# Gated decode block: w_q's few-partition piece in 8 groups of 32 partitions, and a sigmoid made of exponentials

## The chip, the core and the metric

One core of one Trainium2 chip (trn2) runs the whole kernel in one launch. The metric is the device time of an execution in microseconds (us), as the median of several runs. Profiled executions are shown beside it: there the hardware profiler records every instruction and every DMA packet of one execution.

## The reference, cut to what matters

Two rows x (2 x 448) are normalised; one branch is attention of one new token over a cache of 4096 positions, the other a bilinear feed-forward part whose result goes through silu and gates the first.

```python
xn = (x - mean) / sqrt(var + 1e-5)                  # 2 x 448
q = xn @ wq                                         # 448 x 4096: 16 heads of 256, two for each of 8 kv heads
p = softmax(q @ k_cache.T / 16)                     # per row and kv head: 4096 positions of 256
s = (p @ v_cache) @ wo                              # 4096 x 448
g = silu(((xn @ w_gate) * (xn @ w_up)) @ w_down)    # silu(y) = y * sigmoid(y); 448 x 1792, twice, 1792 x 448
out = x + s * g
```

All is float32. The caches are 67 MB each, the weights some 25 MB: every byte is read once, and nearly all of the kernel's traffic is that.

## The kernel before, in words

**Data.** The host lays every input out so that a transfer is 128 partitions with one contiguous row each. There are 16 attention steps i, one for each pair of kv head and row of x; a step needs k_i and v_i, 4 MB each. They come in pairs "v_i k_(i+1)" into a ring of two 8 MB buffers (`ring`). Weights share one slot (`slot`, one buffer): w_q's first half with its extra piece, then w_gate and w_up, w_down with w_q's second half, then w_o. The last transfer (v15 and the last third of w_o, `wo2`) is cut in seven, so that its parts can be used as they land.

**Order of the transfers.** All of these are issued by SP, on one queue, in the order of a list written by hand (`plan`, and `issue`, which takes the next of the list; L78 issues a transfer, L82 the extra piece of w_q). The program calls `issue` behind the work that frees a buffer: the matmuls that read it stand ahead of the issue, and SP waits for them. x's two rows come on ACT's queue (L106).

**Start.** Layernorm of x on DVE (L118 to L130), transposes of xn on TensorE (L133, L155, L156) and copies that repeat a column 16 times for each row of x (L136): `xnT` holds 3 blocks of 128 rows of xn, `xf` the last 64 rows, `xeT` and `xl` pieces of these 64 rows for the extra piece of w_q.

**w_q's first half.** `rows` (L191) multiplies: four column tiles c, each with its own 32 columns of TensorE, and three blocks k of 128 rows (L199). The last 64 rows are folded: `block(12)` holds those of column tiles 0 and 1, 64 partitions each, and `block(13)` those of tiles 2 and 3 (L201). For the first half of w_q, block 12 is left out of the main transfer, which so is 13 x 512 wide, and comes as the piece `wqx`: tiles 0's and 1's 64 rows, as three parts of 20 rows for each (L208) and one of 4 + 4 rows (L211, with `xl`, which two selects of POOL have masked). Its transfer writes 20 partitions, 3584 numbers wide. Its source is made with shape 5 x 5 x 3584, of which `wqx[:, :4]` is read: 5 groups of 4 rows, with an unread row behind each group.

**A step.** `scores(i)` (L274) multiplies q with k_i and takes the maximum (L275); `softmax` (L287 to L298) makes it one maximum for all partitions, then ACT's exponential (L295) and a transpose on DVE; `values(i)` (L313) multiplies with v_i. After steps 0, 2, 4 and 8 a piece of other work is put in: the feed-forward's first half, its second half (`ffn_out`, L253 to L262), w_q's second half, and w_o's first part.

**The gate.** `ffn_out` multiplies with w_down (L256), sums over the tiles (`spread`, L239), and forms gate = y * sigmoid(y) from the 128 x 112 sums: ACT's sigmoid (L261) and a product on DVE (L262). The gate is read at the very end (L422).

**The end.** The last values() (L313, out to a tile `s`) reads v15 in three parts as they land; then ACT scales (L410), TensorE combines (L322) and multiplies with the last parts of w_o (`project`, L351, and `project_last`, L356), DVE multiplies by the gate and adds x (L422, L423), and SP stores the result.

Of the kernel before, what the change touches and what calls it, by code (L numbers as in the profile page):

```python
# [8 lines left out]
F32 = mybir.dt.float32  # L9
AF = mybir.ActivationFunctionType  # L10
OP = mybir.AluOpType
AX = mybir.AxisListType

B, D = 2, 448
HKV, REP, SK, DH = 8, 2, 4096, 256
F = 1792
NT = 4
W = 32
DUP = W // 2
NK = 4  # L20
# [3 lines left out]
SL = D // NT  # L24
# [2 lines left out]
LATE = 24  # L27
THIRD = [24, 25, 26, 28, 29, 30, 31, 27]
PART = 14 * (D + 512)
SIDE = 20  # L30
NS = 3
EXTRA = 2 * NS + 1
LEFT = 64 - NS * SIDE
EPS = 1e-5


# [5 lines left out]
def gated_decode_block(ctx: ExitStack, tc: tile.TileContext, x, first, vk, last0, last1, wq0, wqx, wdq, wo, wgu, out):  # L42
    nc = tc.nc
# [18 lines left out]
    loaded = {}  # L62
    todo = []

    def issue(n=1):
        for names, src, cuts in todo[:n]:
            weight = names[0].startswith("w")
            if weight:
                t = slot.tile([128, PART], F32, name="slot", align_bytes=512)
            else:  # L70
                t = ring.tile([128, 2 * ROW], F32, name="ring", align_bytes=512)
            width = ROW if not weight else src.shape[1] // len(names)
            for i, name in enumerate(names):
                loaded[name] = t[:, i * width:(i + 1) * width]
            if names == ["wd", "wq1"]:
                loaded["wd"], loaded["wq1"] = t[:, :14 * D], t[:, 14 * D:]
            for lo, hi in zip(cuts, cuts[1:]):
                nc.sync.dma_start(t[:, lo:hi], src[:, lo:hi])  # L78
            if names == ["wq0"]:
                at = src.shape[1]  # L80
                loaded["wqx"] = t[:, at:at + EXTRA * 512]
                nc.sync.dma_start(loaded["wqx"][:SIDE], wqx[:, :4])  # L82
        del todo[:n]

# [22 lines left out]
    ident = const.tile([128, 128], F32)  # L107
# [18 lines left out]

    xn = e1[:, 1]
    nc.vector.tensor_scalar(xn[:, :D], xc, rstd, None, op0=OP.mult)  # L128
    nc.vector.tensor_scalar(xn[:, D:D + LEFT], xc[:, D - LEFT:], rstd, None, op0=OP.mult)
    nc.vector.tensor_scalar(xn[:, D + LEFT:], xc[:, 384:D - LEFT], rstd, None, op0=OP.mult)  # L130
    pt = bank()
    for k in range(NK):
        nc.tensor.transpose(pt[:, B * k:B * (k + 1)], xn[:, k * 128:(k + 1) * 128], ident[:B, :B])  # L133
    def copies(dst, pt):
        n, b = pt.shape
        nc.vector.tensor_copy(dst.rearrange("p k (b j) -> p k b j", b=B),  # L136
                              pt.rearrange("p (k b) -> p k b", b=B)[:, :, :, None].to_broadcast([n, b // B, B, DUP]))
# [10 lines left out]
        half = slice(64 * a, 64 * (a + 1))  # L148
        copies(xf[half, a:a + 1], pt[half, (NK - 1) * B:NK * B])

    xeT = spare[:SIDE, :NS]
    pt = bank()
    for j in range(NS):
        at = 384 + j * SIDE
        nc.tensor.transpose(pt[:SIDE, B * j:B * (j + 1)], xn[:, at:at + SIDE], ident[:B, :B])  # L155
    nc.tensor.transpose(pt[:2 * LEFT, B * NS:B * (NS + 1)], xn[:, D - LEFT:D + LEFT], ident[:B, :B])  # L156
    copies(xeT, pt[:SIDE, :NS * B])

    xl = spare[:2 * LEFT, NK + 2:NK + 4]
    for a in range(2):  # L160
        copies(xl[:, a:a + 1], pt[:2 * LEFT, NS * B:(NS + 1) * B])
    nc.gpsimd.affine_select(out=xl, in_=xl, compare_op=OP.is_ge, fill=0.0, base=0, pattern=[[-LEFT, 2], [0, W]],
                            channel_multiplier=1)
    nc.gpsimd.affine_select(out=xl, in_=xl, compare_op=OP.is_ge, fill=0.0, base=LEFT - 1, pattern=[[LEFT, 2], [0, W]],
                            channel_multiplier=-1)

    both = work.tile([128, D], F32, name="h")[:B, :W].rearrange("p (b j) -> p b j", b=B)
    nc.vector.tensor_copy(both, ident[:B, :B, None].to_broadcast([B, B, DUP]))
# [22 lines left out]
    def rows(ps, w, n, extra=None):  # L191


        def block(i):
            return w[:, i * n:(i + 1) * n]

        for k in range(3):
            for c in range(NT):
                nc.tensor.matmul(ps[W * c:W * (c + 1), :n], xnT[:, k, :], block(NT * k + c), start=k == 0, stop=False)  # L199
        def last(a, i):  # L200
            nc.tensor.matmul(ps[64 * a:64 * (a + 1), :n], xf.rearrange("p a j -> p (a j)"), block(i), start=False, stop=True)  # L201

        if extra is not None:

            for j in range(NS):
                for c in range(2):
                    at = (c * NS + j) * n
                    nc.tensor.matmul(ps[W * c:W * (c + 1), :n], xeT[:, j, :], extra[:SIDE, at:at + n], start=False, stop=False)  # L208
                if j == 0:
                    last(1, 12)  # L210
            nc.tensor.matmul(ps[:2 * W, :n], xl.rearrange("p a j -> p (a j)"), extra[:2 * LEFT, 2 * NS * n:(2 * NS + 1) * n],  # L211
                             start=False, stop=True)
            return
        for a in range(2):
            last(a, 12 + a)


    qT = [const.tile([128, B, 4, 2, REP, DUP], F32, name=f"qT{h}") for h in range(2)]
# [33 lines left out]
    def ffn_out():  # L252
        ps = bank()  # L253
        for i in range(14):
            t = i % NT
            nc.tensor.matmul(ps[W * t:W * (t + 1), :D], hT[:, i], loaded["wd"][:, i * D:(i + 1) * D],  # L256
                             start=i < NT, stop=i >= 14 - NT)
        y = bank()
        spread(lift(ps), y, True, True)
        e = work.tile([128, D], F32, name="h")[:, :SL]  # L260
        nc.scalar.activation(e, y[:, :SL], AF.Sigmoid)  # L261
        nc.vector.tensor_mul(gate, y[:, :SL], e)  # L262


    def scores(i):
# [214 lines left out]
```

## Time and profile before

| | before |
|---|---|
| time, median of 3 runs | 376.34 us (376.27 to 376.48) |
| span of the profiled execution, first to last instruction | 374.6 us |
| bytes read from HBM | 158.56 MB, 423 GB/s over the span |
| TensorE: matmul busy, weight load busy | 197.4 us (53%), 55.3 us (15%) |
| DVE, ACT, POOL busy | 72.6, 25.8, 1.7 us |
| mean granted TensorE clock | 0.775 |
| main transfer of w_q's first half; its extra piece | 3328.0 KB; 280.0 KB |

The median is of executions that are timed without the profiler's records; the span is that of one other execution, and leaves out what lies ahead of the program's first instruction and behind its last. In the profile, a line such as "L313 PE MATMUL o<-ring,pT" reads: line 313 of the kernel, on TensorE, writes tile o from tiles ring and pT. "ring", "slot" and "last" are the names of buffers or inputs; buffer numbers are left out. DMA queues are q1 (what SP issues), q10 (what ACT issues), q8 and q14 ("instruction"). The core has sixteen DMA engines; a transfer of 128 partitions is shared by all of them, eight rows each, and a packet is here one row of a transfer.

### The profile page before, as it was taken

How to read it: one execution, taken by the hardware profiler on the slowest of the kernel's cores; microseconds unless marked ns; L12 is line 12 of the kernel's file. 1: busy time of each engine (PE TensorE's matmuls, PEld its weight loads, DVE VectorE, ACT ScalarE, POOL GpSimd, SP SyncE). 2: the span in 40 equal slices, each digit the busy share in tenths (PEclk: the TensorE clock that was granted, in tenths of full speed). 3: DMA queues.
4: the chain of work that ended last, by engine and by line, in shares of the span. 5: the costliest groups of instructions: out<-in, count | busy, mean ns of one | idle time of the engine just before them, and what ended most of it. 6: DMA issues, size and time to landing. Idle time of an engine off the chain costs nothing.

```text
span 374.6 us, 3092 instructions
## 1 busy us (share of the span) xinstructions
PE 197.4 (53%) x1388; PEld 55.3 (15%) x1388; DVE 72.6 (19%) x125; ACT 25.8 (7%) x40; POOL 1.7 (0%) x9
## 2 busy tenths in 40 slices
PE   0793459081726090858271756712718180909785
PEld 0210112020201020212020211200202020202122
DVE  2303030104040003040404050400211212030530
ACT  1001010001020002010101010100010101010121
POOL 0000000000000000000000000000000000000000
PEclk9968596778696587796778696885868586777999
DMA  8999899999999999999999999999999999999994
GB/s 327 435 493 434 376 438 441 448 443 437 431 428 443 441 434 420 422 427 434 436 448 448 427 426 397 452 448 448 436 427 420 436 427 420 448 411 441 411 416 186
DMA packets 4217, 158.81 MB, mean 424 GB/s; under 512 B 599, under 2 KB 857, under 8 KB 1241
## 3 DMA queue, kind: packets, MB, share of 16 engines
q1 hardware_dynamic: 4201, 158.62, 98.2%
q8 instruction: 11, 0.18, 0.2%
q10 hardware_dynamic: 4, 0.00, 0.0%
q14 instruction: 1, 0.01, 0.0%
HBM read 158.56 MB, written 0.06 MB: 423 GB/s over the span
## 4 chain that ended last, share of the span: by engine, by line
DMA 74%; PE 23%; issue 1%; DVE 1%; ACT 0%; POOL 0%; ACTq 0%; SPq 0%; DVEq 0%
DMA ring<-vk 67%; PE o L313 10%; PE s L274 8%; DMA ring<-last 5%; DMA p<-x 2%; PE s L199 1%; PE s L208 1%; PE s L313 1%; PE s L211 1%; PE s L356 0%; PE s L201 0%; PE wide L351 0%; ACT ob L410 0%; PE cb L322 0%; DVE pT L121 0%
## 5 line engine op out<-in xcount | busy, mean ns | idle before, releaser
L313 PE MATMUL o<-ring,pT 128*32 128x512 f32 x480 | 83.2, 856 | 115.6 <-DMA ring<-vk 115.6
L275 DVE TENSOR_REDUCE m<-s 128x1 f32<-128x1024 f32 x16 | 19.6, 1222 | 219.9 <-PE s L274 219.9
L274 PE MATMUL s<-ring,qT 128*32 128x512 f32 x512 | 59.6, 607 | 0.9 <-PE s L211 0.9
L313 PEld LDWEIGHTS o<-ring,pT 128*32 128x32 f32 x480 | 20.8, 150 | 168.6 <-issue 156.1
L295 ACT ACTIVATE p<-s,m 128x1024 f32<-128x1024 f32 x16 | 17.8, 1113 | 286.1 <-DVE m L293 286.1
L274 PEld LDWEIGHTS s<-ring,qT 128*32 128x32 f32 x512 | 17.2, 112 | 40.7 <-issue 38.1
L298 DVE STREAM_TRANSPOSE pT<-p 128x1024 f32<-128x1024 f32 x15 | 18.7, 1245 | 21.2 <-ACT p L295 21.2
L199 PE MATMUL s<-slot,xnT 128*32 128x512 f32 (+1 forms) x96 | 15.3, 788 | 3.3 <-DMA slot<-wgu 3.3
L287 PE MATMUL sm<-ident,m 128*1 128x128 f32 x16 | 4.3, 270 | 18.8 <-DVE m L275 18.8
L289 DVE TENSOR_REDUCE mx<-sm 1x128 f32<-1x512 f32 x16 | 10.7, 671 | 2.9 <-PE sm L287 2.9
L292 PE MATMUL sm<-one,mx 1*128 1x1 f32 x16 | 3.6, 226 | 14.2 <-DVE mx L289 14.2
L373 DVE COPY ob<-o 128x512 f32<-128x512 f32 x14 | 9.5, 681 | 0.0
L256 PE MATMUL s<-slot,hT 128*32 128x448 f32 x28 | 5.8, 918 | 4.4 <-DMA slot<-wdq 4.4
L351 PE MATMUL wide<-slot,oT 128*32 128x448 f32 x48 | 6.4, 684 | 0.7 <-DVE oT L340 0.6
L287 PEld LDWEIGHTS sm<-ident,m 128*1 128x1 f32 x16 | 1.3, 79 | 32.9 <-DVE m L275 32.3
L133 PE MATMUL s<-ident,pT 2*128 2x2 f32 x4 | 0.6, 246 | 10.4 <-DVE pT L128 10.4
L322 PE MATMUL cb<-ob,add_blocks 128*32 128x512 f32 (+2 forms) x48 | 4.1, 456 | 2.4 <-DVE ob L373 1.6
L199 PEld LDWEIGHTS s<-slot,xnT 128*32 128x32 f32 x96 | 3.5, 137 | 11.7 <-issue 11.7
L292 PEld LDWEIGHTS sm<-one,mx 1*128 1x128 f32 x16 | 2.3, 142 | 17.2 <-DVE mx L289 17.2
L295 ACT ACT_TABLE_LOAD x2 | 2.6, 1283 | 30.6 <-DVE m L293 23.5
L313 PE MATMUL s<-ring,slot 128*32 128x512 f32 x32 | 4.2, 600 | 0.8 <-DMA ring<-last 0.8
L201 PE MATMUL s<-slot,oT 128*64 128x448 f32 (+1 forms) x14 | 4.6, 664 | 0.0
(76 smaller groups left out, 47.5 us busy)
## 6 DMA issues: line engine op xcount, KB each, us to landing
ring<-last SPq DMA_DIRECT2D x2, 4096.0 KB, 24.8
slot<-wdq SPq DMA_DIRECT2D x1, 6720.0 KB, 45.5
slot<-wgu SPq DMA_DIRECT2D x1, 6272.0 KB, 32.7
slot<-wo SPq DMA_DIRECT2D x1, 5376.0 KB
ring<-first SPq DMA_DIRECT2D x1, 4096.0 KB, 20.6
slot<-wq SPq DMA_DIRECT2D x1, 3328.0 KB, 10.7
ring<-last SPq DMA_DIRECT2D x1, 2048.0 KB
ring<-last SPq DMA_DIRECT2D x1, 1536.0 KB, 17.8
```

Source lines behind the costliest of these rows:

```text
L199: nc.tensor.matmul(ps[W * c:W * (c + 1), :n], xnT[:, k, :], block(NT * k + c), start=k == 0, stop=False)
L256: nc.tensor.matmul(ps[W * t:W * (t + 1), :D], hT[:, i], loaded["wd"][:, i * D:(i + 1) * D], start=i < NT, stop=i >= 14 - NT)
L274: nc.tensor.matmul(s[W * c:W * (c + 1), h, :], q[:, d], k[:, h, d, c, :], start=d == 0, stop=d == 1)
L275: nc.vector.tensor_reduce(m[:, 0:1], s, axis=AX.XY, op=OP.max)
L287: nc.tensor.transpose(sm[:1, :128], m[:, 0:1], ident)
L289: nc.vector.tensor_reduce(mx, sm[:1, None, :128].rearrange("p o (c j) -> p o j c", c=NT).to_broadcast([1, NT, W, NT]), axis=AX.X, op=OP.max)
L292: nc.tensor.transpose(sm[:, 128:129], mx.rearrange("p c j -> p (c j)"), one)
L295: nc.scalar.activation(p, s, AF.Exp, bias=m[:, 1:2], scale=1.0 / 16, accum_out=su[:, place(i):place(i) + 1])
L298: nc.vector.transpose(pT.rearrange("p h n -> p (h n)"), p.rearrange("p h n -> p (h n)"))
L313: nc.tensor.matmul(o[W * t:W * (t + 1), :], pT[:, h, at:at + 2 * W:2], loaded[f"v{i}"][:, e * 512:(e + 1) * 512], start=e < NT, stop=e >= ...
L351: nc.tensor.matmul(wide[W * t:W * (t + 1), :D], heads(oT, i, first), w, start=i < NT, stop=i >= SIDES - NT)
L373: nc.vector.tensor_copy(ob[:, place(i) % 8], o)
```

## The change

- **The piece of w_q.** `SIDE` goes from 20 to 32 partitions, so the piece has 8 groups of 4 rows. It holds the last 64 rows of all four column tiles (two parts of 32 rows each) and, of block 11 (rows 256 to 383 of xn, column tile 3), the right half: 256 columns, as four parts of 32 rows. Its row is 5120 numbers. The main transfer of w_q's first half becomes 12 x 512 - 256 = 5888 numbers wide: blocks 12 and 13 and the half block are gone from it. No zeros are sent any more in place of rows that a part lacks.
- **Its operands and matmuls.** Six transposes of 32 rows each (two for the last 64 rows, four for rows 256 to 383) take the place of three of 20 and one of 8. `xl`, its two copies and POOL's two selects go. In `rows`, the last of the twelve main matmuls writes 256 columns; four matmuls of 256 columns and eight of 512 follow. Before it was twelve, six of 20 rows, one of block 13 and one of 4 + 4 rows.
- **The fold of the other weights** no longer rolls tiles 1's and 3's rows by four.
- **The gate.** With m = min(y, 0): sigmoid(y) = exp(m) / (1 + exp(2m - y)), where 2m - y is -|y|. DVE makes m and 2m - y side by side (128 x 112 each), ACT takes the exponential of both in one instruction, and DVE adds one, takes the reciprocal, and multiplies twice. ACT's program has one table load in place of three.

```diff
--- before.py
+++ after.py
@@ -27,10 +27,11 @@
 LATE = 24
 THIRD = [24, 25, 26, 28, 29, 30, 31, 27]
 PART = 14 * (D + 512)
-SIDE = 20
-NS = 3
-EXTRA = 2 * NS + 1
-LEFT = 64 - NS * SIDE
+SIDE = 32
+NS = 64 // SIDE
+HALF = 256
+QUARTERS = 128 // SIDE
+EXTRA = NT * NS * 512 + QUARTERS * HALF
 EPS = 1e-5
 
 
@@ -78,7 +79,7 @@
                 nc.sync.dma_start(t[:, lo:hi], src[:, lo:hi])
             if names == ["wq0"]:
                 at = src.shape[1]
-                loaded["wqx"] = t[:, at:at + EXTRA * 512]
+                loaded["wqx"] = t[:, at:at + EXTRA]
                 nc.sync.dma_start(loaded["wqx"][:SIDE], wqx[:, :4])
         del todo[:n]
 
@@ -126,8 +127,7 @@
 
     xn = e1[:, 1]
     nc.vector.tensor_scalar(xn[:, :D], xc, rstd, None, op0=OP.mult)
-    nc.vector.tensor_scalar(xn[:, D:D + LEFT], xc[:, D - LEFT:], rstd, None, op0=OP.mult)
-    nc.vector.tensor_scalar(xn[:, D + LEFT:], xc[:, 384:D - LEFT], rstd, None, op0=OP.mult)
+    nc.vector.tensor_scalar(xn[:, D:], xc[:, 384:], rstd, None, op0=OP.mult)
     pt = bank()
     for k in range(NK):
         nc.tensor.transpose(pt[:, B * k:B * (k + 1)], xn[:, k * 128:(k + 1) * 128], ident[:B, :B])
@@ -148,21 +148,12 @@
         half = slice(64 * a, 64 * (a + 1))
         copies(xf[half, a:a + 1], pt[half, (NK - 1) * B:NK * B])
 
-    xeT = spare[:SIDE, :NS]
+    xeT = spare[:SIDE, 6:6 + QUARTERS + NS]
     pt = bank()
-    for j in range(NS):
-        at = 384 + j * SIDE
+    for j in range(QUARTERS + NS):
+        at = 256 + j * SIDE
         nc.tensor.transpose(pt[:SIDE, B * j:B * (j + 1)], xn[:, at:at + SIDE], ident[:B, :B])
-    nc.tensor.transpose(pt[:2 * LEFT, B * NS:B * (NS + 1)], xn[:, D - LEFT:D + LEFT], ident[:B, :B])
-    copies(xeT, pt[:SIDE, :NS * B])
-
-    xl = spare[:2 * LEFT, NK + 2:NK + 4]
-    for a in range(2):
-        copies(xl[:, a:a + 1], pt[:2 * LEFT, NS * B:(NS + 1) * B])
-    nc.gpsimd.affine_select(out=xl, in_=xl, compare_op=OP.is_ge, fill=0.0, base=0, pattern=[[-LEFT, 2], [0, W]],
-                            channel_multiplier=1)
-    nc.gpsimd.affine_select(out=xl, in_=xl, compare_op=OP.is_ge, fill=0.0, base=LEFT - 1, pattern=[[LEFT, 2], [0, W]],
-                            channel_multiplier=-1)
+    copies(xeT, pt[:SIDE, :(QUARTERS + NS) * B])
 
     both = work.tile([128, D], F32, name="h")[:B, :W].rearrange("p (b j) -> p b j", b=B)
     nc.vector.tensor_copy(both, ident[:B, :B, None].to_broadcast([B, B, DUP]))
@@ -196,23 +187,20 @@
 
         for k in range(3):
             for c in range(NT):
-                nc.tensor.matmul(ps[W * c:W * (c + 1), :n], xnT[:, k, :], block(NT * k + c), start=k == 0, stop=False)
-        def last(a, i):
-            nc.tensor.matmul(ps[64 * a:64 * (a + 1), :n], xf.rearrange("p a j -> p (a j)"), block(i), start=False, stop=True)
-
+                part = HALF if extra is not None and (k, c) == (2, NT - 1) else n
+                nc.tensor.matmul(ps[W * c:W * (c + 1), :part], xnT[:, k, :], w[:, (NT * k + c) * n:(NT * k + c) * n + part], start=k == 0, stop=False)
         if extra is not None:
-
+            for j in range(QUARTERS):
+                at = NT * NS * n + j * HALF
+                nc.tensor.matmul(ps[W * (NT - 1):, HALF:n], xeT[:, j, :], extra[:SIDE, at:at + HALF], start=False, stop=False)
             for j in range(NS):
-                for c in range(2):
+                for c in range(NT):
                     at = (c * NS + j) * n
-                    nc.tensor.matmul(ps[W * c:W * (c + 1), :n], xeT[:, j, :], extra[:SIDE, at:at + n], start=False, stop=False)
-                if j == 0:
-                    last(1, 12)
-            nc.tensor.matmul(ps[:2 * W, :n], xl.rearrange("p a j -> p (a j)"), extra[:2 * LEFT, 2 * NS * n:(2 * NS + 1) * n],
-                             start=False, stop=True)
+                    nc.tensor.matmul(ps[W * c:W * (c + 1), :n], xeT[:, QUARTERS + j, :], extra[:SIDE, at:at + n], start=False,
+                                     stop=j == NS - 1)
             return
         for a in range(2):
-            last(a, 12 + a)
+            nc.tensor.matmul(ps[64 * a:64 * (a + 1), :n], xf.rearrange("p a j -> p (a j)"), block(12 + a), start=False, stop=True)
 
 
     qT = [const.tile([128, B, 4, 2, REP, DUP], F32, name=f"qT{h}") for h in range(2)]
@@ -257,9 +245,15 @@
                              start=i < NT, stop=i >= 14 - NT)
         y = bank()
         spread(lift(ps), y, True, True)
-        e = work.tile([128, D], F32, name="h")[:, :SL]
-        nc.scalar.activation(e, y[:, :SL], AF.Sigmoid)
-        nc.vector.tensor_mul(gate, y[:, :SL], e)
+        e = work.tile([128, D], F32, name="h")
+        up, low = e[:, :SL], e[:, SL:2 * SL]
+        nc.vector.tensor_scalar(up, y[:, :SL], 0.0, None, op0=OP.min)
+        nc.vector.scalar_tensor_tensor(low, up, 2.0, y[:, :SL], op0=OP.mult, op1=OP.subtract)
+        nc.scalar.activation(e[:, :2 * SL], e[:, :2 * SL], AF.Exp)
+        nc.vector.tensor_scalar(low, low, 1.0, None, op0=OP.add)
+        nc.vector.reciprocal(low, low)
+        nc.vector.tensor_mul(gate, y[:, :SL], up)
+        nc.vector.tensor_mul(gate, gate, low)
 
 
     def scores(i):
@@ -445,7 +439,7 @@
 
         full = w[:384].reshape(3, 128, NT, n).transpose(1, 0, 2, 3).reshape(128, 12, n)
         last = w[384:].reshape(64, 2, 2, n).transpose(2, 0, 1, 3)
-        last = np.concatenate([last[0], np.roll(last[1], LEFT, 0)])
+        last = np.concatenate([last[0], last[1]])
         return np.concatenate([full, last], 1).reshape(128, 14 * n)
 
 
@@ -453,14 +447,11 @@
     wq0, wq1 = [folded(wq[:, h], 512) for h in range(2)]
 
 
-    wqx = np.zeros((SIDE // 4, 5, EXTRA * 512), np.float32)
-    t0, t1 = wq0[:64, 12 * 512:13 * 512], wq0[64:, 12 * 512:13 * 512]
-    ends = np.zeros((SIDE, EXTRA, 512), np.float32)
-    ends[:, :NS] = t0[:NS * SIDE].reshape(NS, SIDE, 512).transpose(1, 0, 2)
-    ends[:, NS:2 * NS] = t1[LEFT:].reshape(NS, SIDE, 512).transpose(1, 0, 2)
-    ends[:2 * LEFT, 2 * NS] = np.concatenate([t0[NS * SIDE:], t1[:LEFT]])
-    wqx[:, :4] = ends.reshape(SIDE // 4, 4, EXTRA * 512)
-    wq0 = np.concatenate([wq0[:, :12 * 512], wq0[:, 13 * 512:]], 1)
+    wqx = np.zeros((SIDE // 4, 5, EXTRA), np.float32)
+    ends = wq[384:, 0].reshape(NS, SIDE, NT, 512).transpose(1, 2, 0, 3)
+    half = wq[256:384, 0, 4 * 512 - HALF:].reshape(QUARTERS, SIDE, HALF).transpose(1, 0, 2)
+    wqx[:, :4] = np.concatenate([ends.reshape(SIDE, -1), half.reshape(SIDE, -1)], 1).reshape(SIDE // 4, 4, EXTRA)
+    wq0 = c(wq0[:, :12 * 512 - HALF])
     wo = np.asarray(A_wo).reshape(NC, 128, D)[[*range(LATE), *THIRD]]
     wo = wo.transpose(1, 0, 2).reshape(128, NC * D)
     wo, last[1] = c(wo[:, :LATE * D]), np.concatenate([last[1], wo[:, LATE * D:]], 1)
```

## What I predicted

> **What bounds the kernel now.** I read the page first, then stretches of time, then the chain of waits.
>
> ```profile
> span 374.6 us, 3092 instructions
> PE 197.4 (53%) x1388; PEld 55.3 (15%) x1388; DVE 72.6 (19%) x125; ACT 25.8 (7%) x40; POOL 1.7 (0%) x9
> DMA packets 4217, 158.81 MB, mean 424 GB/s; under 512 B 599, under 2 KB 857, under 8 KB 1241
> q1 hardware_dynamic: 4201, 158.62, 98.2%
> q8 instruction: 11, 0.18, 0.2%
> q14 instruction: 1, 0.01, 0.0%
> DMA 74%; PE 23%; issue 1%; DVE 1%; ACT 0%; POOL 0%; ACTq 0%; SPq 0%; DVEq 0%
> ```
>
> No engine is busy for much over half of the span; SP's queue (q1) fills 98.2% of sixteen DMA engines, and 74% of the last chain is transfers. The stretches (columns: us, granted clock, share of the 16 engines, GB/s):
>
> ```profile
> 13.00:40.00 27.00, 0.79 1.03 445
> 40.00:365.00 325.00, 0.76 1.00 431
> 366.00:367.00 1.00, 1.00 1.02 420
> 367.62:368.90 1.28, 1.00 0.82 328
> 368.90:369.65 0.75, 1.00 0.58 222
> 369.65:370.20 0.55, 1.00 0.23 88
> 370.20:370.80 0.60, 1.00 0.08 30
> ```
>
> For 325 us all sixteen are full, at 431/16 = 26.9 GB/s each, so 1 us is 26.9 KB on one engine. At the end they do **not** stop together: the share falls to 0.82 (13 engines), 0.58 (9), 0.23 (4), 0.08 (1). A transfer has landed when its slowest engine has, so the others' spare time at the end is lost.
>
> Which engine stops late, and why, comes from the packets themselves. An engine's next packet starts where its last one ended (3 to 4 ns apart in the records), so 4201 packets fall into sixteen strings. No view prints these; I chained the trace's packet records, and numbers below that have no row are from there. The trace doesn't number the engines; grouped by what each carries, the strings end (us):
>
> ```
> carries                        strings  v's middle piece ends         last wo2 piece ends
> a w_q piece                       4     364.05 364.07 364.15 364.27   369.68 369.71 369.79 369.91
> a w_q piece, 8 KB instructions    1     364.67                        370.30
> neither                           3     361.98 362.00 362.23          367.62 367.64 367.87
> 16 KB instructions once           6     363.33 to 363.99              368.97 to 369.63
> 16 KB instructions twice          2     364.72 365.13                 370.36 370.77
> ```
>
> The few-partition piece of w_q is cut in 5 groups and lies on five strings, four packets of 14,336 B each. q8's first ten packets fall on eight other strings, in turn (the ninth and tenth on those of the first and second). Each leaves a hole of 0.86 to 0.95 us and makes the packet behind it some 0.5 us longer: 1.4 us. Three strings have neither.
>
> Does the end hang on the slowest string? The chain of waits, in order of time (start, us, what):
>
> ```profile
> 307.23 30.44 DMA ring<-vk
> 337.81 6.01 PE o L313 x32
> ...
> 347.69 17.79 DMA ring<-last
> 365.52 2.30 PE s L313 x16
> ...
> 370.09 0.78 PE s L356 x24
> 370.88 0.19 PE s L239 x8
> 371.07 0.47 PE s L356 x16
> ```
>
> And the timeline of PE ahead of the wait (start, us, ..., idle before and what ended it):
>
> ```profile
> 362.81 1.93 PE L313 MATMUL s<-ring,slot 128*32 128x512 f32 x16
> 365.52 2.28 PE L313 MATMUL s<-ring,slot 128*32 128x512 f32 x16 [0.79 <-DMA ring<-last]
> ```
>
> Yes, twice. The second half of the last values() waits 0.79 us for v's middle piece, whose last string ends at 365.13. The last eight passes of project_last start at 371.1, 0.33 us after the last string ends at 370.77; PE gets there at the same moment by the other way. Both instants are the slowest string's, and what follows (to 374.6) is fixed work.
>
> **The change part by part.**
>
> *w_q's piece.* Per string, main w_q goes from 8 x 26,624 B to 8 x 23,552 B: 24,576 B less, **-0.91 us** for all sixteen. The piece is now 32 rows of 20,480 B in 8 groups of 4: +81,920 B, +3.04 us, on eight strings. I take these to be the five that have a piece (which lose 57,344 B, 2.13 us) and the three that have nothing:
> - five with a piece: -0.91 - 2.13 + 3.04 = 0.00. Last end 370.30, the others by 369.91.
> - three with nothing: -0.91 + 3.04 = +2.13: 369.75, 369.77, 370.00.
> - eight with instructions: -0.91: 369.86 and 369.45 where there are two packets, the rest under 368.8.
>
> That the three new ones are these and not three others is the one premise. Five groups lay on five strings that had no q8 packet though eight of the sixteen had; q8 walks round a closed set of eight. [...]
>
> *The gate's sigmoid* (i = 2, after the fourth softmax). ACT loses two table loads; DVE has six operations in place of one:
>
> ```profile
> L295 ACT ACT_TABLE_LOAD x2 | 2.6, 1283 | 30.6 <-DVE m L293 23.5
> 109.30 1.28 ACT L261 ACT_TABLE_LOAD   x1
> ...
> 142.97 1.28 ACT L295 ACT_TABLE_LOAD   x1 [23.52 <-DVE m L293]
> ...
> 119.49 0.28 DVE L262 TENSOR_TENSOR gate<-s,h 128x112 f32<-128x112 f32 x1 [0.90 <-ACT h L261]
> 140.02 1.23 DVE L275 TENSOR_REDUCE m<-s 128x1 f32<-128x1024 f32 x1 [20.25 <-PE s L274]
> ...
> 140.01 29.93 DMA ring<-vk
> ```
>
> Five more at 0.28 us are 1.4 us, and DVE idles 20.25 us behind them: nothing. The load that returns to the exponential at 142.97 frees 1.28 us of softmax 4, whose reader waits for v4 until 169.94 by the chain: nothing. With those covers gone it would be +1.4 and -2.6 us.
>
> One thing could count. In 0 to 373 us there is one q14 packet:
>
> ```profile
> q14 instruction: 1, 0.01, 19.3%
> ```
>
> This is the stretch 108.70 to 108.80. It is 8,192 B at 108.75, 0.55 us ahead of the sigmoid's table load, and lies on the string that ends at 370.30: a hole of 0.30 us and a packet 0.53 us longer, 0.83 us. Without it that string ends at 369.47, and the three strings at up to 370.00 are last. If it belongs to the table load it goes; if it holds instructions of some engine, it stays. For "goes": the place, and that no other such packet is in the run. For "stays": the other two table loads have none; PE's 2776 recorded instructions took 11 packets of 16,384 B, 252 each, so 8,192 B are 126 instructions, and DVE runs 125 that are counted: about one such block must be fetched for it in the run, whatever ACT does. DVE has one instruction more after the change and three or four fewer ahead of this point, so its block would come as many DVE instructions later, at the same price. [...] Bounds: 0 (stays) and -0.30 us (goes). I take **0**: the count of instructions is nearer than one coincidence in time.
>
> *query(0).* Two transposes and six matmuls more, one of them half as wide, some with 32 rows; POOL's two selects go.
>
> ```profile
> 12.97 5.28 PE s L199 x24
> 22.36 1.91 PE s L211 x2
> 24.27 0.91 issue
> 25.18 5.36 PE s L274 x32
> 30.56 45.70 DMA ring<-vk
> ...
> 24.29 0.34 SPq L78 DMA_DIRECT2D slot<-wgu  x1
> ```
>
> Three rounds over four tiles took 5.28 us, 1.76 each. Now: three rounds (5.3), four half-width matmuls in one tile (at most half of 1.91 each, 3.8), two rounds of the last rows (3.5): 12.6 us against 11.3 from 12.97 to 24.27, so +1.3 at most, and below it down to -2 if the half blocks overlap. Behind it, SP's issue of w_gate/w_up moves from 24.29 to 25.6; the first string is through with v0 at 39.4, so 13 us cover it, and the vk issue at 30.56 is wanted at 54. DMA keeps full (1.03 in 13 to 40 us): nothing. PE's 24 instructions more move each q8 packet six matmuls earlier, on the same strings; ten still fall ahead of the end.
>
> *Sum.* The last string ends at 370.30 in place of 370.77: **-0.47 us**; v's middle piece at 364.67 in place of 365.13: -0.46. PE's first half of that values() ends at 364.74, so up to 0.78 us it is no new wait, and it starts from vk's last landing, which moves by the same. The profiled execution's span goes from 374.6 to 374.1. The median of the runs, 376.34, is 1.7 above the span, for what lies around it; the same difference gives **375.87**.
>
> **The rivals.**
> 1. *The 8 KB packet goes with the table load.* The last string is then 370.00: -0.77, **375.57**. For and against as above.
> 2. *The three newly loaded strings carry q8 packets.* That decides as soon as one of them does. The price is on that string: one with one packet goes to 369.63 + 2.13 = 371.76 (+0.99, 377.33), the worst with two to 372.90 (+2.13, **378.47**), and the end would wait there alone. Against: five of five avoid the eight so far, and just three are left. For: the trace has no engine numbers.
> 3. *It doesn't do what it says: the piece is spread over all sixteen.* 655,360 B / 16 = 40,960 B, 1.52 us each: the string with two packets goes to 370.77 - 0.91 + 1.52 = 371.38, +0.61, **376.95**. Against: 5 groups went to 5.
>
> **How the numbers follow.** Forecast 0.54, rival 1 0.35, rival 2 0.07, rival 3 0.04. Start times of the strings differ by over 1 us (first packets 1.8 to 3.3 us) and single packets by up to 0.08, so an end of one string is good to about 0.15 us. Predicted 375.87; range **375.4 to 376.1**: from rival 1 less 0.15 to the forecast plus 0.2; rivals 2 and 3 (0.11) and tails lie outside. 0.2% is 0.75 us, about what a measurement here can tell from no change: below 375.59 lies half of rival 1 and little else, 0.24; above 377.09 rival 2, 0.07; between, 0.69.
>
> **What would show it.** Right: 32 packets of 20,480 B, on eight strings, none of them with a 16 KB packet; shares at the end of 0.9 to 369.4 and then a steep fall; last string at 370.2 to 370.4; the wait ahead of the second half of values() still put down to a DMA, with PE ahead of it 0.5 us earlier. The q14 packet tells the forecast from rival 1: present behind 108.75, or gone, with the last string at 370.0. Wrong: a 20,480 B string with a 16 KB hole that ends past 371; a hole in the strings between 13 and 365 us that no instruction packet explains; or PE, not DMA, ahead of the last two waits.

## The result, and the profile after

The changed kernel takes **376.88 us** (median of 16 runs, 376.51 to 378.25) where the kernel before, run beside it, takes 376.23 us (16 runs, 376.00 to 376.90): a ratio of **1.0026, 95% interval 1.0018 to 1.0034**. It is slower by a quarter of a per cent; 375.87 had been predicted, with a range of 375.4 to 376.1. The 16 runs stand in two groups with nothing between them: nine at 376.51 to 376.88 and seven at 377.82 to 378.25. That split turns out to be part of the answer. The profiled execution is of the lower group: its own time is 376.88, its span 375.0 (before: 376.34 and 374.6).

The page of the changed kernel, the lines that answer to those shown of before:

```profile
span 375.0 us, 3108 instructions
PE 195.8 (52%) x1398; PEld 57.1 (15%) x1398; DVE 74.2 (20%) x127; ACT 23.4 (6%) x38; POOL 1.3 (0%) x7
DMA packets 4232, 158.78 MB, mean 423 GB/s; under 512 B 602, under 2 KB 860, under 8 KB 1244
q1 hardware_dynamic: 4216, 158.59, 98.1%
q8 instruction: 11, 0.18, 0.2%
q14 instruction: 1, 0.01, 0.0%
DMA 78%; PE 20%; issue 0%; SPq 0%; ACT 0%; DVE 0%
```

As many bytes, the same eleven q8 packets, the 8 KB packet of q14 still there, no engine much nearer to full (DVE 74.2 us for 72.6, weight loads 57.1 for 55.3, matmuls 195.8 for 197.4), and transfers hold more of the last chain (78% for 74%). Nothing here says why it is slower. The stretches do (columns: us, granted clock, share of the sixteen DMA engines, GB/s):

```profile
13.00:40.00 27.00, 0.76 1.02 441
40.00:365.00 325.00, 0.74 1.00 432
366.00:367.00 1.00, 1.00 1.02 420
367.62:368.90 1.28, 1.00 0.75 301
368.90:369.65 0.75, 1.00 0.62 241
369.65:370.20 0.55, 1.00 0.23 88
370.20:370.80 0.60, 1.00 0.16 60
370.80:371.20 0.40, 1.00 0.11 40
```

Up to 367 us the shares of the two profiles differ by 0.01 at most. A share of 0.9 had been forecast up to 369.4; instead it is 0.75 and then 0.62 (before: 0.82 and 0.58). After that, 0.16 x 16 = 2.6 and 0.11 x 16 = 1.8 strings go on, to 371.18, where before it was 0.08 x 16 = 1.3 and one string that ended last, at 370.77. Two strings are late, not one.

The same packet records as before, chained end to start, show which two (no view prints this; us):

```
carries                                 strings  middle piece of v ends     last wo2 piece ends
w_q piece only                             5     364.06 to 364.21           369.69 369.77 369.83 369.85 369.85
w_q piece, 8 KB instructions (110.91)      1     364.84                     370.48
w_q piece, 16 KB instructions once         2     365.49 365.54              371.13 371.18
nothing                                    2     -                          366.77 367.30
16 KB instructions once                    4     -                          368.22 368.26 368.32 368.57
16 KB instructions twice                   2     -                          369.23 369.51
```

The piece lies on eight strings as the diff says. Two of the eight are among those that carry PE's instruction packets (at 263.80 and 287.89 us, each with its hole of 0.86 us). The three that were to be filled up were not the three empty ones: two strings still have nothing, so only one of those three got the piece.

Does the end still hang on the last string? The chain of waits of the changed kernel, in order of time (start, us, what):

```profile
347.15 18.75 DMA ring<-last
365.94 2.31 PE s L307 x16
...
370.52 0.78 PE s L350 x24
371.30 0.19 PE s L227 x8
371.49 0.51 PE s L350 x16
```

and its timeline of PE (start, us, ..., idle before and what ended it; L307 is before's L313):

```profile
362.38 1.92 PE L307 MATMUL s<-ring,slot 128*32 128x512 f32 x16
365.94 2.29 PE L307 MATMUL s<-ring,slot 128*32 128x512 f32 x16 [1.65 <-DMA ring<-last]
```

PE arrives 0.43 us earlier than before (362.38 for 362.81) and starts the second half 0.42 us later (365.94 for 365.52): its idle time ahead of v's middle piece goes from 0.79 to 1.65 us. The last string's end moves by the same amount, 371.18 - 370.77 = +0.41, and so does the span, +0.4. From the last string's end to the kernel's time it is 376.34 - 370.77 = 5.57 us before and 376.88 - 371.18 = 5.70 after. That constant, 5.6 to 5.8 us, held in each of the nine experiments whose strings were read to the end, so one string's end gives the time.

### The profile page after: what moved, and what is told of

The parts are those of the page before. It is cut to its first block, busy times and chain, and to the rows that moved or that the text cites. A ratio compares the mean times of both kernels' runs of the same rounds, so it can differ in the third digit from the quotient of the medians.

```text
span 375.0 us, 3108 instructions
## 1 busy us (share of the span) xinstructions
PE 195.8 (52%) x1398; PEld 57.1 (15%) x1398; DVE 74.2 (20%) x127; ACT 23.4 (6%) x38; POOL 1.3 (0%) x7
## 4 chain that ended last, share of the span: by engine, by line
DMA 78%; PE 20%; issue 0%; SPq 0%; ACT 0%; DVE 0%
DMA ring<-vk 68%; PE o L307 11%; PE s L268 8%; DMA ring<-first 5%; DMA ring<-last 5%; PE s L307 1%; PE s L350 0%; SPq L83 0%; PE wide L345 0%; ACT ob L404 0%; PE cb L316 0%; SPq L79 0%; PE sm L300 0%; DVE gate L416 0%; DVE gate L417 0%
## 5 line engine op out<-in xcount | busy, mean ns | idle before, releaser
L307 PE MATMUL o<-ring,pT 128*32 128x512 f32 x480 | 84.2, 865 | 115.2 <-DMA ring<-vk 115.2
L307 PEld LDWEIGHTS o<-ring,pT 128*32 128x32 f32 x480 | 21.3, 150 | 168.0 <-issue 150.9
L191 PE MATMUL s<-slot,xnT 128*32 128x448 f32 (+2 forms) x96 | 16.3, 830 | 2.2 <-DMA slot<-wgu 2.2
L244 PE MATMUL s<-slot,hT 128*32 128x448 f32 x28 | 4.9, 811 | 5.4 <-DMA slot<-wdq 5.4
L316 PE MATMUL cb<-ob,add_blocks 128*32 128x512 f32 (+2 forms) x48 | 5.4, 575 | 2.4 <-DVE ob L367 1.6
L345 PE MATMUL wide<-slot,oT 128*32 128x448 f32 x48 | 4.9, 543 | 1.6 <-DMA slot<-wo 1.1
L307 PE MATMUL s<-ring,slot 128*32 128x512 f32 x32 | 4.2, 599 | 1.8 <-DMA ring<-last 1.6
L287 DVE TENSOR_SCALAR m<-sm 128x1 f32<-128x1 f32 x16 | 2.5, 159 | 5.1 <-PE sm L286 5.1
L212 DVE STREAM_TRANSPOSE qT<-s 128x256 f32<-128x256 f32 x4 | 1.6, 428 | 10.0 <-PE s L199 7.3
```

The costliest lines, as they stand in the source:

```text
L191: nc.tensor.matmul(ps[W * c:W * (c + 1), :part], xnT[:, k, :], w[:, (NT * k + c) * n:(NT * k + c) * n + part], start=k == 0, stop=False)
L307: nc.tensor.matmul(o[W * t:W * (t + 1), :], pT[:, h, at:at + 2 * W:2], loaded[f"v{i}"][:, e * 512:(e + 1) * 512], start=e < NT, stop=e >= ...
L316: nc.tensor.matmul(cb[W * c:W * (c + 1), :n * 64], add_blocks[:, e].rearrange("p r j -> p (r j)"), src[:, :n, e, :, c, :], start=e == 0, s ...
```

## The experiments

Theory after the result: the time is the end of the slowest string; every term of the sum has its predicted size, and only the assignment was wrong. Two engines carry both the piece and PE's 16 KB packets, and which engines get a second such packet differs from run to run; that makes the two groups. Rivals: the gate's exponentials cost time; the piece costs something besides its bytes; the two groups are a disturbance that has nothing to do with the kernel. None of the ten kernels leaves out any of the reference's work; e5 and e6 add matmuls, and e1 and e7 transfers, that nothing reads. A string is called doubled below when two 16 KB instruction packets fell on it, and the round is the set of engines on which these packets fall in turn.

### e2_gate_only: the gate's edit in the kernel before

```
-        e = work.tile([128, D], F32, name="h")[:, :SL]
-        nc.scalar.activation(e, y[:, :SL], AF.Sigmoid)
-        nc.vector.tensor_mul(gate, y[:, :SL], e)
+        up, low = e[:, :SL], e[:, SL:2 * SL]
...
+        nc.scalar.activation(e[:, :2 * SL], e[:, :2 * SL], AF.Exp)
...
```

> The kernel before with the gate made of exponentials alone. Theory (the piece of w_q costs, the gate nothing): as before, 376.2 us within 0.2, and the 8,192-byte packet is still there without a table load in the run. Rival (the gate's DVE work or a shift in the programs costs the difference): 376.9 us, slower by 0.6.

Measured: 376.28 (11 runs) beside 376.29 (21 runs), ratio 1.0003 (0.9994 to 1.0011). The profile of e2, ACT's table loads in its groups, and q14 in 0 to 373 us:

```profile
L301 ACT ACT_TABLE_LOAD x1 | 1.3, 1283 | 7.2 <-DMA p<-x 7.2
```

```profile
q14 instruction: 1, 0.01, 0.0%
```

One table load is left, in the kernel's first microseconds; the two around the gate are gone. The 8 KB packet is still there, at 110.86 us. So the gate's edit changes the time by no more than some 0.1% either way, and the packet does not belong to the gate's table loads.

### e3_piece_only: the changed kernel with its old sigmoid

```
-        nc.scalar.activation(e[:, :2 * SL], e[:, :2 * SL], AF.Exp)
...
+        nc.scalar.activation(e, y[:, :SL], AF.Sigmoid)
+        nc.vector.tensor_mul(gate, y[:, :SL], e)
```

> The changed kernel with the table's sigmoid back, so the new piece alone. Theory: as the changed kernel, most runs at 376.5 to 376.9 and a second group at 377.8 to 378.3, last string 371.2. Rival (the gate costs): 376.2 us in one group.

Measured: 376.67 (11 runs: eight from 376.58 to 376.85, then 377.20 and 378.18, and one of 411.71 at a granted clock of 1.0, which nothing here explains), ratio 1.0015 (1.0005 to 1.0024). The end of its DMA, columns as above:

```profile
370.20:370.60 0.40, 1.00 0.17 63
370.60:370.90 0.30, 1.00 0.13 48
```

Again two strings (0.13 x 16 = 2.1) go on alone, to 370.88 and 370.97, and they are two with the piece and one 16 KB packet each, here at 156.6 and 176.0 us instead of 263.8 and 287.9. The round of the q8 packets had started three strings further on. So the piece alone makes the loss, and the round does not start at the same string in every profiled run. The run of 377.20 lies between the two groups; it has no trace.

### e1_numbers and e7_numbers: which engine is which

The trace does not number engines. If a transfer of a few rows, n, leaves packets on n strings, and these are nested, small transfers of different n tell the strings apart. e1 puts fourteen of them (2 to 15 rows) behind the first vk:

```
+    probe = qT[1].rearrange("p b g d r j -> p (b g d r j)")
+    at = 0
+    for n in range(2, 16):
+        nc.sync.dma_start(probe[:n, at:at + 4 * n], first[:n, :4 * n])
+        at += 4 * n
```

> The changed kernel with fourteen tiny transfers behind the first vk (2 rows of 8 numbers, 3 rows of 12, up to 15 rows of 60, so packets of 32 to 240 bytes), which number the strings: string number e carries those of more than e rows. Nothing else changes, so about 376.9 or 378.0 us as the changed kernel shows. Theory (the piece now shares engines with instruction packets): the 20,480-byte packets lie on strings 0 to 7, two of the strings 5 to 7 carry a 16 KB packet each and end last (371.2 us), the eight strings with 16 KB packets are neighbours in number, and the two strings that end first (366.8, 367.3) have numbers over 7. Rival (the piece is not on the lowest strings, or instruction packets are dealt out anew in every program): the 16 KB packets are on strings without order, or not on 5 to 7.

Measured: 383.44 us; the probe was too large. The packets of the transfers of nine and more rows moved only at 43.2 to 45.8 us, and w_gate/w_up came behind them. SP's instructions on line 79 from 20 to 60 us (duration ns min/median/max, first and last start):

```profile
L79 SPq EVENT_SEMAPHORE  x4: 17/17/10471, 45.0 to 52.3; - x4
L79 SPq DMA_DIRECT2D slot<-wgu x1: 352/352/352, 45.0 to 45.0; - x1
```

In the changed kernel the slot<-wgu issue is at 21.28; here it is at 45.0, and everything behind it is late. Its time says nothing. Its strings could be read only in part: number 5 carried two 16 KB packets and number 6 one.

e7 keeps six of them:

```
+    for n in (5, 6, 7, 13, 14, 15):
```

> The changed kernel with six tiny transfers behind the first vk (5, 6, 7, 13, 14 and 15 rows: packets of 80, 96, 112, 208, 224, 240 bytes), few enough that SP isn't held up; 376.5 to 378.3 us. They tell string 5 (96 and 112 but not 80), 6 (112 alone of these), 7 (none of these three, but the piece), and 13, 14, 15. Theory: strings 6 and 7 carry instructions and 5 does not, and the two strings with nothing are 14 and 15, so that the round is 6 to 13. Rival: another two of 5 to 7, or a round that is not of neighbours.

Measured: 378.50 us, one run. The strings, by number (us):

```
number      piece   16 KB packets at         last wo2 piece ends
0 to 4      yes     none (one has 8 KB)
5           yes     two: 80.76, 355.92       372.71
6           yes     one: 106.97              371.08
7           yes     none                     369.83
8 to 12     no      one each on four; none on one (367.02)
13          no      one: 290.07
14          no      two: 46.27, 327.54       369.73
15          no      none                     367.96
```

The detail of my expectation was wrong: 5 and 6 carry packets, not 6 and 7, and the round isn't a block of neighbours. In time order the packets went to 14, 5, 6, four of 8 to 12, 13, and again to 14 and 5. The numbers are those of the probes: the transfers of 5, 6, 7, 13, 14 and 15 rows had packets on as many strings, each smaller one's strings were among the next one's, and the piece's eight groups lay on the strings so numbered 0 to 7.

This run is of the upper group, and shows how that comes about: string 5 carries the piece and **two** 16 KB packets. The end of e7's DMA:

```profile
370.80:371.10 0.30, 1.00 0.09 36
371.10:372.70 1.60, 1.00 0.06 25
```

From 371.10 on one single string (0.06 x 16 = 1) runs, for 1.6 us, until 372.7; the kernel's time, 378.50, is 5.79 us behind its end at 372.71.

### e5_after_more_instr and e6_before_more_instr: every engine of the round gets two

If the groups come from which engines get a second packet, then a kernel that fetches sixteen of them before the end, two for each of the eight engines, must have one group: the upper one with the change, and without it the upper end of before's spread. Both kernels add 32 one-element matmuls to twelve softmaxes (the page of e5 counts 768 matmuls and 768 weight loads more, 1536 instructions on PE):

```
+        if 1 <= i <= 12:
+            for n in range(32):
+                nc.tensor.matmul(sm[:1, 256 + n:257 + n], one, one, start=True, stop=True)
```

> The changed kernel with 32 tiny matmuls more in each of the softmaxes 1 to 12, whose results nobody reads: 1536 instructions of TensorE, six 16 KB packets more, 16 in all ahead of the end, so that each of the eight strings that carry them has two wherever the round starts. Theory (the two groups of runs of the changed kernel are starts of the round at different strings, the slow ones where a string with the piece has two packets): one group of runs, at the height of the slow one, last string 371.18 + 1.41 = 372.6, 378.0 to 378.3 us, and the two piece strings with instructions last in the trace. Rival (the instruction packets are not what holds the end): 376.5 to 376.9 and now and then 378, as without them.

> The kernel before with the same tiny matmuls. Theory: every one of its eight instruction strings has two packets; last is the one that starts latest, 369.63 + 1.41 = 371.0 in place of 370.77: 376.3 to 376.9 us. Rival (the matmuls themselves or their traffic delay the end): as much slower as the changed kernel gets by them, 1.3 us or more.

Measured, e5: 378.14 (four runs, 378.04 to 378.23), ratio 1.0051 (1.0034 to 1.0068); e6: 376.81 (ten runs, 376.62 to 376.89), ratio 1.0013 (1.0003 to 1.0022). One narrow group each. The page of e5, its q8 line, and the end of its DMA:

```profile
q8 instruction: 17, 0.28, 0.3%
```

```profile
371.00:371.40 0.40, 1.00 0.11 45
371.40:372.60 1.20, 1.00 0.12 46
```

Two strings (0.12 x 16 = 1.9) go on together to 372.54 and 372.57, where the theory had 372.6 for the piece and two packets. The same stretch of e6, the kernel before with as many packets:

```profile
371.00:371.40 0.40, 1.00 0.05 18
```

One string, to 371.29: it carries no piece, but is the latest from the start (its w_q was through at 11.43 us, the others' at 10.3 to 10.9). That would place before's own spread too, 376.0 to 376.3 in most runs and 376.6 to 376.9 in some, by whether the late string is among the doubled ones; no slower run of the kernel before was traced, so this is not shown, and three of its runs beside e9 (376.96 to 377.20) lie above that. The 1536 instructions moved nothing that these strings do not account for. The rival "a disturbance" falls: with more instructions all four runs are in the upper group, and the trace shows both late strings doubled.

### e4_four_groups: the same bytes on four strings

```
-                nc.sync.dma_start(loaded["wqx"][:SIDE], wqx[:, :4])
+                nc.sync.dma_start(loaded["wqx"][:SIDE], wqx[:, :8])
...
-    wqx = np.zeros((SIDE // 4, 5, EXTRA), np.float32)
+    wqx = np.zeros((SIDE // 8, 9, EXTRA), np.float32)
```

> The changed kernel with the same piece in 4 groups of 8 rows in place of 8 groups of 4: the same bytes, blocks and matmuls, on four strings. Theory (each string's time is its bytes at 26.9 GB/s and 1.4 us for each 16 KB of instructions): the four carry 163,840 bytes, 6.08 us in place of 3.04, and end at 372.8 (373.5 if the 8 KB packet lies there), the strings with instructions at 368 to 370: 378.5 to 379.2 us, in one group of runs, since none of the four has a 16 KB packet. Rival (the new layout costs by something other than the share of the strings, such as longer rows or more matmuls): 376.9 us with two groups of runs as now.

Measured: 385.18 us (385.09 to 385.40), ratio 1.0237 (1.0222 to 1.0253). One group of runs, as expected, since no string has both; but the size missed by 6 us. The stretch of w_q in e4, and beside it the one in the changed kernel:

```profile
12.00:20.00 8.00, 1.00 0.97 204
```

```profile
9.60:12.20 2.60, 1.00 1.05 454
```

All engines are occupied (0.97), yet they move 204 GB/s for 454: the packets themselves take longer. Of the 32 packets of 20,480 B, 24 took 1.56 to 1.63 us and eight 0.84 to 1.38, where each takes 0.76 in the changed kernel, and packets of k on other strings took up to 2.6 us where 1.21 is usual. The four piece strings ended at 378.82 to 379.58. What differs besides the number of strings is, by the shapes, which rows of the piece go together: four groups of eight neighbouring rows instead of eight groups of four.

### e8_rows_64: the piece on other partitions

To test whether the place where the packets land is what costs, the piece keeps its eight groups but lands on partitions 64 to 95 instead of 0 to 31, and DVE copies it to 0 to 31:

```
-                nc.sync.dma_start(loaded["wqx"][:SIDE], wqx[:, :4])
+                nc.sync.dma_start(loaded["wqx"][64:64 + SIDE], wqx[:, :4])
...
+        if h == 0:
+            nc.vector.tensor_copy(loaded["wqx"][:SIDE], loaded["wqx"][64:64 + SIDE])
```

> The changed kernel with the piece landed on partitions 64 to 95 and copied to 0 to 31 by DVE at the start. In the four-group run each packet of the piece took 1.6 us in place of 0.76. Theory A (a packet is slow when it writes partitions that another engine's packets write at the same time): each packet takes 1.5 us or more here too, the eight strings end 3 us later, some 380 us. Theory B (it was the 8 rows in a group, or four strings alone): 0.76 us each and 376.9 or 378 us as the changed kernel.

Measured: 381.27 us, one run. The stretch of its w_q piece:

```profile
9.60:14.00 4.40, 1.00 1.09 236
```

Half the rate of the changed kernel's 454 GB/s at full occupancy (1.09), as in e4, with eight strings and packets of 20,480 B as in that kernel; these took 1.5 to 1.6 us (the first ones 0.89 to 1.2). The last string, with the piece and two 16 KB packets, ended at 375.55, 3 us behind the 372.5 to 372.7 of such a string in e5 and e7. In the transfer only the partitions differ, so here it is where the packets land that makes them slow: 1.5 to 1.6 us for 0.76. Why is not shown: no trace here tells which engine writes which row, so theory A's reason stays open, and so does whether e4's packets, as slow, are so for the same one. In the changed kernel the packets have full speed (0.76 us for 20,480 B, 26.9 KB per us). The rival "costs something besides its bytes" falls for the change as it stands.

### e9_two_tiles: eight groups with less in them

The piece holds the last 64 rows of two column tiles only, 32 rows of 8,192 B, and the main part is 26,624 B as before:

```
-EXTRA = NT * NS * 512 + QUARTERS * HALF
+EXTRA = 2 * NS * 512
```

> The changed kernel with less in the piece: the last 64 rows of column tiles 0 and 1 alone, 32 rows of 2048 numbers in 8 groups, and the rest of those rows and the half block back in the main transfer, which is as wide as before (6656). So the piece holds what it held before, on eight strings in place of five, 32,768 B (1.22 us) on each. Theory (what hurts is the piece on strings that carry instructions): strings 0 to 4 end 0.9 us earlier than before, 7 at 368.9, 5 and 6 at 370.2 with one packet and 371.6 with two; where the round starts elsewhere the last string is the one of before (370.4 to 371.3) and the time is that of before, 376.0 to 376.9; where 5 or 6 has two packets, three starts in eight, 377.1 to 377.3. Rival (the amount on the strings is what hurt, so a smaller piece heals it): 376.0 to 376.9 in all runs, none over 377. Other rival (the layout of 32 rows in 8 groups costs in itself): 376.5 or more in the fast group.

Measured: 376.89 (12 runs: five at 376.02 to 376.19, two at 376.87 and 376.92, five at 377.16 to 377.45) beside 376.32 (23 runs), ratio 1.0007 (0.9997 to 1.0017). The profiled run is of the upper ones (377.45); the end of its DMA, and then its timeline of PE at the second half of values():

```profile
370.00:371.20 1.20, 1.00 0.09 36
371.20:371.80 0.60, 1.00 0.06 24
```

```profile
366.71 2.27 PE L306 MATMUL s<-ring,slot 128*32 128x512 f32 x16 [1.66 <-DMA ring<-last]
```

One string goes on alone from 370.56, where a doubled string without the piece ends, to 371.82; it has the piece and two 16 KB packets (371.6 expected), while the other string with both, with one packet, ends at 370.07 (370.2 expected) and piece strings without 16 KB packets at 368.55 to 369.54. Same mechanism, smaller size; the upper runs are up to 0.15 us above the 377.1 to 377.3 expected. The five low runs are as fast as the kernel before and no faster.

### e10_after_again: the changed kernel once more

No edit; a fresh set of runs.

> The changed kernel as it is, for a second trace and more runs. Theory (the round of instruction packets starts at a string that changes from run to run): two groups, five starts in eight at 376.5 to 376.9 with the last string at 371.1 to 371.2, three in eight at 377.8 to 378.3 with string 5 or 6 at 372.5 to 372.7. Rival (the second group is some other disturbance of those sessions): one group, or a slow run whose trace shows no piece string with two 16 KB packets.

Measured: 376.87 (12 runs: eight at 376.64 to 376.95, four at 377.82 to 378.33), ratio 1.0020 (1.0009 to 1.0031); the profiled run of 376.83 had its last two strings, with the piece and one packet each, at 371.08 and 371.12. Over both sets 17 runs are low and 11 high. With eight places to start, ten packets and so two neighbours doubled, three of the eight starts double 5 or 6 by e7's order: 17.5 to 10.5 would be expected of 28 if all starts were as likely, which no run shows. The two traces of the changed kernel itself are both of the lower group, with 5 and 6 seventh and eighth in the round. That its own upper runs have 5 or 6 doubled is inferred from e5, e7 and e9, whose upper traces show it; no upper run of the unaltered changed kernel was traced, so the rival's slow run without a doubled piece string is not ruled out there.

## Why the prediction was wrong

**The step that failed** is the one that the prediction called "the one premise": "That the three new ones are these and not three others". It had inferred from five of five strings avoiding the eight with q8 packets that the round lies above the piece's engines, so that groups six to eight would fall on the three empty ones. e7 shows the round as 5, 6, four of 8 to 12, 13 and 14. Five groups (0 to 4, if they nest as e7's do) just miss it; of the three new ones, 5 and 6 are in it and only 7 was empty. Five of five was true, but it says something of 0 to 4 alone. The expectation of e1 and e7, that the round is a block of neighbours, was a second form of the same mistake.

**Rival 2 was the right one**, with 0.07. It was sized at its worst string (369.63 + 2.13 = 371.76). The two strings that were in fact hit stood at 368.97 and 368.98 in before; 368.97 + 2.13 = 371.10, and 371.13 and 371.18 were measured, where 370.30 had been forecast for the last string. It also stopped at one trace: two packets on a newly loaded string was given as "the worst", 378.47, when it is what three of the eight starts would give (upper group, 377.8 to 378.3).

**Could the profile of before have shown it?** In part. In before's packets, two of the six strings with one 16 KB packet have holes of 0.859 and 0.860 us, where the other four and the doubled ones have 0.90 to 0.95; the two of the changed kernel that also have the piece show the same short holes, so these must be 5 and 6, and they keep them (0.86 to 0.87) in every trace but for one hole of 0.91 in e7. So two strings of the eight stood apart in before, but nothing there tied them to the numbers 5 and 6. What would have told is a transfer of six or eight groups, and before has none.

**Point by point, the rest:**
- *w_q's piece*: both sizes hold. Strings without it ended earlier by what -0.91 says or somewhat more (the doubled ones at 369.23 and 369.51, forecast 369.45 and 369.86). Of those with it, the old ones came out even (369.69 to 369.85 beside 369.68 to 369.91 before), and the two that carry 16 KB packets ended 2.16 and 2.20 later, for +2.13.
- *The 8 KB packet stays*: right, 0 taken, 370.48 for 370.30 forecast; rival 1 (0.35) falls with e2. The reason was not right in its detail: that the packet would come "as many DVE instructions later" is not borne out. It came at 108.75 to 122 us, in kernels with and without the gate's edit. Whose instructions it holds stays open.
- *The gate*: nothing, by e2. One of the five added operations is not 0.28 us; DVE's rows in the changed kernel:

```profile
118.57 0.28 DVE L250 TENSOR_SCALAR h<-s 128x112 f32<-128x112 f32 x1 [0.60 <-PE s L227]
...
119.86 0.85 DVE L254 RECIPROCAL h<-h 128x112 f32<-128x112 f32 x1
```

- *query(0)*: it has four matmuls more, not six (the page counts 1398 on PE for 1388, transposes included), and became 3 us shorter, not up to 1.3 longer or 2 shorter. SP's issue behind it, 24.29 before:

```profile
21.28 0.34 SPq L79 DMA_DIRECT2D slot<-wgu  x1
```

  It brings nothing, because the strings are full all the while (a share of 1.02 from 13 to 40 us): the cover named there held in the other direction too.
- *The sum and the bound*: a transfer, not PE, ends the wait ahead of the second half of values() (1.65 us), as forecast; only the string is another. At the last passes of project_last no view names a transfer. Of the signs that were to show the prediction wrong, the first came: "a 20,480 B string with a 16 KB hole that ends past 371".

No version here beats the kernel before. By an estimate from the ends of the strings (370.77 and 370.30 in before), the best split over five groups would gain some 0.15 us, 0.04%; it wasn't tried, since a measurement would not show it. Left open: which of 8 to 12 carries no instruction packets, what decides where the round starts, whether every start occurs, and the run of 411.71 in e3.

## What to carry to other kernels

When the transfers of a kernel fill all the engines (here a share of 1.00 from 40 to 365 us), bytes that go to few of them must be weighed against what those very engines carry besides (here 1.41 us for each 16 KB instruction packet); which engines these are is a fact to be measured, with transfers of 5, 6, 7, ... rows, before a sum is built on it. An inference from what the present layout avoids holds for the present layout. And where the runs of one kernel stand in groups, look in several traces for what moves from run to run: the median of such a kernel depends on how many runs of each group happen to be drawn, and a single profile shows one case of several.

## What the runs showed of the hardware

- PE's 16 KB instruction packets went in rotation over eight engines that aren't neighbours (5, 6, four of 8 to 12, 13 and 14 in e7), from a start that differed between the traces. Each cost its full engine 1.41 us (in the traces read here, a hole of 0.86 to 0.96, and a following packet about 0.5 longer). A packet is 16,384 B for 252 recorded instructions (2776 and 11 packets in before), and 1536 instructions more on PE came with six packets more (17 for 11, e5). Where the engine that carries it is full to the end, the 1.41 us is not hidden: the two late strings ended at 372.54 and 372.57 with two such packets (e5), and at 371.13 and 371.18 with one (the changed kernel).
- Most of the same 20,480 B packets took 1.5 to 1.6 us instead of 0.76 when the piece lay on partitions 64 to 95 (e8), or on 0 to 31 by four engines instead of eight (e4), and packets of k on other strings were slowed up to 2.6 us (e4).
- With fourteen small transfers at once SP was held up: it issued w_gate/w_up at 45.0 us, at 21.28 without them, and the packets of those of nine and more rows moved at 43.2 to 45.8 us, 0.35 to 0.45 us apart from one transfer to the next (e1). With six the time was 378.50 us, beside 377.82 to 378.33 of the upper group without them (e7).
- RECIPROCAL on 128x112 took 0.85 us in the changed kernel, the other DVE operations of that size 0.21 to 0.28.
